# Two score groups set side by side and three transposes moved to the DMA crossbar, in an RWKV-5 and feed-forward kernel on one core

## The chip, the core and the metric

The kernel runs on one core of a Trainium2 chip. A core has five engines with instruction streams of their own: TensorE (PE in the profile; its weight loads are PEld), VectorE (DVE), ScalarE (ACT), GpSimd (POOL) and SyncE (SP), which here only issues DMAs. The metric is the device time of one execution in microseconds (us); lower is better. A change is told by the median of several runs.

## What is computed

Inputs are r, k, v of 4 batches x 8 heads x 768 steps x 48 (float32), w and u (8 x 48), and the two weights of the feed-forward part (384 x 2048 and 2048 x 384).

```python
for t in range(S):                     # per batch and head; state is 48 x 48
    cur = outer(u * k[t], v[t])
    y[t] = r[t] @ (state + cur)
    state = w[:, None] * state + outer(k[t], v[t])
x = y of all heads side by side        # 3072 tokens x 384
h = maximum(x @ w_in, 0)
out = (h * h) @ w_out                  # 3072 x 384, float32
```

## The kernel before

The 4 x 768 tokens are cut into 24 units of 128 tokens of one batch, all 8 heads in each. The list `UNITS` gives unit i's batch and its place in time. Units 0 to 3 are worked in pairs by code of their own (`PAIRED = 4`); the text is about units 4 to 23. The recurrence within a unit is done as matmuls: scores r k^T with the decays multiplied in beforehand, masked, times v, plus r times the state that the batch's earlier unit left.

For a unit i the steps are these (the letter after the colon in `ORDER` names the engine: A ScalarE, D VectorE, G GpSimd, P TensorE, S SyncE):

- `ld.r`, `ld.k`, `ld.v` (L321): loads from HBM, one DMA each.
- `rh`, `kh` (L340, L337): r and k times their decays, into the two halves of tile rk, bf16.
- rk transposed into tile rkT, in one of two ways. Either `T` (L398, eight 128x128 transposes on TensorE into a PSUM bank) and `Tc` (a copy from the bank, L251 on ScalarE, L253 on VectorE); or `XB` (L404), one DMA that turns the tile through the DMA crossbar. Before the change units 4, 5 and 9 go by `T`, the other seventeen by `XB`.
- `A` (L411): eight matmuls with 48 rows each, two rows groups of the array in turn, into two PSUM banks. `Bm` (L419, VectorE, two per unit): the banks times the mask, into Bm.
- `P0`, `P1`, `du`, `dv` (L343, L347, L350, L355): the term with u, kept apart from the matmuls. `vb` (L251 or L253): v in bf16.
- `Y` (L450, L452): state times r and Bm times v, into a bank. `xs` (L475, VectorE): that plus dv, in bf16.
- `U` (L463), `ts`, `S` (L481, L484): the state's step.
- xs transposed into its half of the group's tile xT, again in one of two ways. Either `X` (L489, three transposes on TensorE) and `xTc` (a copy from the bank, L251 or L253); or `xX` (L496), one DMA through the crossbar. Before the change units up to 15 go by `X`, units 16 to 23 by `xX`.

The feed-forward part works on groups of one or two units (`GROUPS`: units 4 and 5 are group 3, 8 and 9 group 5, 12 and 13 group 7, 14 and 15 group 8). `F1.g.s` (L505, six matmuls of 128x256 or twelve of 128x128) makes a bank of x @ w_in, `re` (L515 on ScalarE, L517 on VectorE) takes the maximum with 0, `sq` (L522, L524) squares. `F2.i.q` (L533, four matmuls of 128x384) adds a quarter of the second product into a bank of unit i, `os` copies it out of the bank, and `out.i` (L586; L584 for the paired units) stores it, one DMA. Unit 23 is done in column parts (`Fh`, `oh`, `outh`).

What sets the order of the work is one string, `ORDER`. Its words are emitted one after the other, each on its engine, so that every engine's instruction stream is `ORDER` filtered by its letter; nothing is reordered later. After the engine's letter stand the buffers that the step fills: `A.5:P/6/0` puts unit 5's scores into PSUM banks 6 and 0. Waits between engines follow from the tiles and banks that steps share. DMAs of the letters S, A and G are issued by SyncE, ScalarE and GpSimd. SyncE issues nearly all; a step behind a waiting one on its queue waits too.

Of the kernel before, what the change touches and what calls it, by code (L numbers as in the profile page):

```python
# [51 lines left out]
kh.11:D/3 X.7:P/4 U.7:P/5 kh.10:G/5 F2.4.2:P/0 xTc.7:A/2 ts.7:D/0 XB.11:S/2 vb.8:A/0 F1.4.1:P/4 os.4:A/4 S.7:D
F1.4.7:P/5 re.4.1:A/3 P0.10:D/1 du.9:D/3 XB.8:S/3 U.8:P/0 F2.5.2:P/6 re.4.7:A/4 vb.9:G/1 S.6:D F1.4.3:P/4 os.5:A/5
XB.10:S/4 P1.8:D re.4.3:D/0 F1.4.4:P/5 F1.4.0:P/6 re.4.4:A/2 rh.13:D/4 ld.k.13:S/4 F1.4.2:P/4 ts.8:D/0 ld.v.11:S/2
re.4.0:A/5 sq.4.1:D/24 U.9:P/5 ld.v.10:S/3 F1.4.5:P/0 re.4.2:A/1 ts.9:D/1 sq.4.0:A/25 sq.4.3:D/26 A.11:P/1/2 A.9:P/6/4
P0.11:D/2 P1.11:G sq.4.2:A/27 F2.6.0:P/5 ld.r.12:S/4 Bm.9.1:D/2 re.4.5:A/3 F2.6.1:P/5 sq.4.7:A/5 Bm.9.0:D/3
ld.v.12:S/4 dv.9:G sq.4.5:A/7 Bm.11.1:D/5 F1.4.6:P/4 Bm.11.0:D/7 sq.4.4:A/3 du.8:D/4 kh.13:G/4 A.10:P/3/7 A.8:P/0/6
re.4.6:A/5 F2.7.0:P/2 Bm.8.0:D/0 sq.4.6:A/9 ld.k.12:S/5 ld.r.15:S/7 Y.9:P/1 dv.8:D vb.11:A/2 F2.7.2:P/2 Bm.8.1:D/1
S.9:G vb.10:A/3 ld.k.14:S/7 F2.6.3:P/5 out.4:A P1.10:G Y.8:P/4 xs.9:D/3 F2.7.3:P/2 xs.8:D/4 P0.13:G/0 X.9:P/0
Bm.10.1:D/4 X.8:P/6 F2.6.2:P/5 xTc.8:A/0 du.11:D/0 xTc.9:D/0 rh.12:G/0 Y.11:P/1 U.10:P/4 du.10:D/2 dv.10:G out.0:S  # L60
F1.5.7:P/7 dv.11:G Bm.10.0:D/6 F1.5.6:P/6 ld.v.13:S/5 re.5.7:A/0 P1.13:D ld.r.14:S/6 F1.5.3:P/0 xs.11:D/0 re.5.6:A/1
# [10 lines left out]
rh.17:G/1 F2.10.1:P/6 re.6.4:A/2 xs.12:D/2 F2.11.0:P/2 os.9:D/1 sq.6.4:A/21 P0.16:G/0 XB.17:S/3 ts.13:D/1 Y.13:P/1
kh.16:D/5 F2.10.3:P/6 rh.16:G/5 F2.10.2:P/6 xs.13:D/3 out.5:S du.15:D/4 ld.k.18:S/4 F2.10.0:P/6 P1.16:G ld.r.21:S/3
A.15:P/7/5 A.14:P/0/3 ld.r.19:S/2 Bm.15.0:D/5 dv.15:G X.12:P/1 F2.11.1:P/2 ld.r.18:S/5 Bm.15.1:D/7 S.13:G X.13:P/7
F2.11.3:P/2 xTc.12:D/2 xTc.13:A/2 Bm.14.0:D/4 Y.15:P/5 vb.14:G/7 du.14:D/0 F1.7.3:P/1 ld.v.16:S/1 kh.19:G/0 xs.15:D/4
F1.7.2:P/7 re.7.3:A/0 Bm.14.1:D/6 F1.7.6:P/0 out.9:S out.6:S os.8:D/3 re.7.2:A/1 ld.r.20:S/4 sq.7.3:D/17 Y.14:P/5
re.7.6:A/3 P0.21:G/3 dv.14:D du.17:D/2 F1.7.1:P/1 XB.16:S/2 os.10:A/4 X.15:P/3 F1.7.4:P/4 S.12:G xTc.15:D/0 xs.14:D/0
F1.7.5:P/7 ld.k.20:S/5 rh.19:G/0 U.15:P/0 F1.7.7:P/6 re.7.5:A/4 ld.v.17:S/0 ts.15:D/1 X.14:P/3 S.15:G F1.7.0:P/5
re.7.7:A/5 xTc.14:D/0 P0.19:D/2 sq.7.2:A/20 sq.7.6:A/22 F1.8.7:P/7 XB.19:S/4 F1.8.6:P/0 re.7.4:D/2 sq.7.7:A/23
U.14:P/6 rh.21:G/3 out.8:A F1.8.5:P/3 re.8.6:D/0 kh.18:G/4 ld.r.23:S/6 vb.16:A/1 du.16:D/3 F1.8.0:P/4 sq.7.5:A/24  # L80
rh.20:G/6 re.7.0:D/1 F1.8.2:P/0 re.8.7:A/3 rh.18:D/4 ld.v.19:S/3 sq.7.4:A/25 F1.8.4:P/5 re.8.2:A/5 sq.8.2:A/5
# [555 lines left out]
```

## Time and profile before

| | us |
|---|---|
| median of 3 runs | 170.87 (170.55 to 171.42) |
| the profiled execution | 171.19 |
| its span, first to last instruction | 169.5 |
| TensorE busy | 164.2 |
| VectorE busy | 137.1 |
| ScalarE busy | 101.9 |
| GpSimd busy | 99.9 |

The profile is of one execution. The span is what its views cover; about 1.7 us of the execution's own time lie around it. A row of a timeline has the start (us from the span's start), the duration, engine, line, operation, what it writes and reads, and how many instructions were merged into the row. Where a bracket ends the row, it has the idle time of the engine ahead of it and what ended that. Rows of TensorE carry modelled ends that overlap the next row's start. The busy share of an engine is an average over the whole; the 40 slices show it in time, each digit a tenth.

### The profile page before, as it was taken

The page shows a single profiled execution, that of the slowest core. Times are in us where ns is not written, and L with a number is a line of the kernel's source. Part 1 is how long each engine was busy: PE and PEld are TensorE (multiplying, and loading weights), DVE is VectorE, ACT ScalarE, POOL GpSimd, SP SyncE. Part 2 cuts the span into 40 slices and gives each one's busy share as a digit, 9 for nine tenths or more (in the row PEclk, how much of TensorE's full clock was granted, in tenths as well). Part 3 has the DMA queues.
Part 4 walks back from the last instruction along what each step waited for, and adds up shares of the span by engine and source line. Part 5 has one row for each costly group of instructions (what it writes and reads, how often), then busy time and mean ns, then how long its engine had stood idle before and what let it go on. Part 6 is the DMA issues. An engine that isn't in the chain of part 4 may idle for free.

```text
span 169.5 us, 4602 instructions
## 1 busy us (share of the span) xinstructions
PE 164.2 (97%) x1828; PEld 125.4 (74%) x1828; DVE 137.1 (81%) x255; ACT 101.9 (60%) x190; POOL 99.9 (59%) x122
## 2 busy tenths in 40 slices
PE   4999999999999999999999999999999999999993
...
DMA packets 96137, 27.56 MB, mean 163 GB/s; under 512 B 90642, under 2 KB 96020, under 8 KB 96116
## 3 DMA queue, kind: packets, MB, share of 16 engines
...
q0 software_dynamic: 2816, 3.54, 11.5%
...
q8 instruction: 14, 0.23, 0.6%
q14 instruction: 7, 0.06, 0.1%
...
## 4 chain that ended last, share of the span: by engine, by line
PE 95%; ACT 1%; DVE 1%; issue 1%; ACTq 0%
PE bank L505 37%; PE bank L533 36%; PE bank L411 3%; PE bank L463 2%; PE bank L452 2%; PE bank L364 2%; PE bank L489 2%; PE bank L450 2%; PE bank L547 2%; PE bank L440 1%; PE bank L269 1%; DVE Bm L392 1%; PE bank L303 1%; PE bank L272 1%; PE bank L398 1%; PE bank L428 1%
## 5 line engine op out<-in xcount | busy, mean ns | idle before, releaser
L505 PE MATMUL bank<-xT,W 128*128 128x256 bf16 (+1 forms) x672 | 70.0, 257 | 0.0
L533 PE MATMUL bank<-W,hq 128*128 128x384 bf16 x368 | 68.9, 326 | 0.0
L505 PEld LDWEIGHTS <-W 128*128 128x128 bf16 x672 | 56.9, 98 | 7.7
L515 ACT ACTIVATE hr<-bank 128x512 bf16<-128x512 f32 x67 | 38.7, 594 | 36.4 <-PE bank L505 27.8
L533 PEld LDWEIGHTS <-hq 128*128 128x128 bf16 x368 | 33.8, 98 | 18.2
L522 ACT ACTIVATE hq<-hr 128x512 bf16<-128x512 bf16 x70 | 41.0, 626 | 3.4 <-DVE hr L517 2.8
L419 DVE TENSOR_TENSOR Bm<-bank,maskJT 128x512 bf16<-128x512 f32 x40 | 25.7, 682 | 2.7 <-PE bank L411 2.7
L355 POOL TENSOR_TENSOR dv<-ldv,du 128x384 f32<-128x384 f32 (+1 forms) x18 | 15.9, 891 | 16.2 <-DVE du L350 11.3
L517 DVE TENSOR_SCALAR hr<-bank 128x512 bf16<-128x512 f32 x29 | 19.7, 686 | 6.6 <-PE bank L505 4.5
L347 POOL TENSOR_TENSOR P<-P,ub 128x384 f32<-128x384 f32 x15 | 16.0, 1070 | 13.1 <-DVE P L343 12.7
L340 POOL TENSOR_TENSOR rk<-ldr,Wt 128x384 bf16<-128x384 f32 x15 | 16.4, 1101 | 0.0
L343 POOL TENSOR_TENSOR P<-ldr,ldk 128x384 f32<-128x384 f32 x13 | 13.3, 1023 | 1.5 <-DMA ldk<-in_k_dram 1.2
L524 DVE TENSOR_TENSOR hq<-hr 128x512 bf16<-128x512 bf16 x26 | 12.4, 490 | 2.0 <-ACT hr L515 1.8
L484 POOL TENSOR_TENSOR S0W<-ts,WLm 128x384 bf16<-128x384 f32 x10 | 10.9, 1091 | 4.4 <-DVE ts L481 3.6
L475 DVE TENSOR_TENSOR xs<-bank,dv 128x384 bf16<-128x384 f32 x20 | 11.1, 553 | 3.0 <-PE bank L452 1.1
L337 POOL TENSOR_TENSOR rk<-ldk,Wk 128x384 bf16<-128x384 f32 x12 | 12.3, 1032 | 1.4 <-DMA ldk<-in_k_dram 1.4
L350 DVE TENSOR_REDUCE du<-P 128x8 f32<-128x384 f32 x24 | 12.9, 542 | 0.0
L253 DVE COPY os<-bank 128x384 f32<-128x384 f32 x11 | 6.1, 551 | 6.9 <-PE bank L533 6.9
L481 DVE TENSOR_TENSOR ts<-bank,S0W 128x384 f32<-128x384 f32 x16 | 8.7, 550 | 1.2 <-POOL S0W L484 0.8
L452 PE MATMUL bank<-vb,Bm 128*128 128x48 bf16 x160 | 9.5, 183 | 0.0
L251 ACT COPY os<-bank 128x384 f32<-128x384 f32 (+2 forms) x14 | 6.3, 458 | 4.5 <-PE bank L533 2.5
L452 PEld LDWEIGHTS <-Bm 128*128 128x128 bf16 x160 | 8.2, 96 | 1.0
...
## 6 DMA issues: line engine op xcount, KB each, us to landing
...
```

The source lines that it names most:

```text
L340: e.tensor_mul(rk[slot[f"rk{i}"]][:, 0, :, 0:D], loaded("r", i), Do.factor("t", i % 2 if i < PAIRED else 2))
L343: e.tensor_mul(P0b[slot[f"P{i}"]], loaded("r", i), loaded("k", i))
L347: e.tensor_mul(t, t, bank("bu")[:, 0 : H * D].rearrange("p (h d) -> p h d", h=H) if i in EARLY_U else ub)
L350: e.tensor_reduce(dub[slot[f"dv{i}"]], P0b[slot[f"P{i}"]], axis=mybir.AxisListType.X, op=ALU.add)
L355: e.tensor_mul(dv_of(i) if i < PAIRED else dvb[slot[f"dv{i}"]], loaded("v", i), t)
L419: e.tensor_mul(Bmb[slot[f"Bm{i}{h}"]], heads(bank(f"bA{i}{h}"), 128), mask_b)
L452: e.matmul(y[:, hc, D * h : D * (h + 1)], m[h][:, hc, :], vb[:, 2 * hc + h, :], start=(c == 0), stop=True, skip_group_check=True,)
L505: e.matmul(hp[:, fi, :], W1[f // 4][:, c, 256 * (f // 2 % 2) : 256 * (f // 2 % 2 + 1)].rearrange("p (m j) -> p j m", j=2)[:, f % 2, :], xt ...
L515: e.activation(hr, hp, AF.Relu)
L517: e.tensor_scalar_max(hr, hp, 0.0)
L522: e.activation(hq, hr, AF.Square)
L533: e.matmul(bank(f"bO{i}")[:, 0:d_model], hqb[slot[f"hq{g},{f // m}"]][:, at : at + L], W2[q][:, f % 4, :], start=(seen[i] == 1 and f % 4 = ...
```

## The change

Only words of `ORDER` change; no function does.

- `A.5` stands right behind `A.4`, in banks 1 and 2 instead of 6 and 0. `A.6` stands right behind `A.7`, in banks 1 and 2 instead of 6 and 5, and `Bm.6.0`, `Bm.6.1` stand right behind `Bm.7.0`, ahead of `re.3.5` and `P1.9` on VectorE.
- Unit 9's r and k: `T.9` and `Tc.9` go, `XB.9` comes, on SyncE behind `ld.v.8`, into the same buffer.
- The x of units 12 and 15: `X.12`, `xTc.12`, `X.15`, `xTc.15` go; `xX.12` and `xX.15` come, on SyncE, each behind the unit's `xs` in `ORDER`.
- The stores `out.12`, `out.15` and `out.16` go from SyncE's queue to GpSimd's, at the same places in `ORDER`.

The diff, with the string's line breaks moved so that each part is seen by itself:

```diff
 P1.4:D du.4:D/4 sq.1.1:D/9 A.4:P/5/0
+A.5:P/1/2
 sq.2.6:A/10 re.2.3:A/5 sq.2.3:A/11 F2.0.1:P/4 sq.2.0:A/12 F2.0.3:P/4 vb.4:G/4 Bm.4.1:D/0 Bm.4.0:D/1 sq.2.7:A/13 P0.5:D/1
-A.5:P/6/0
 Bm.5.1:D/2 sq.2.4:A/14 F2.1.1:P/5 Bm.5.0:D/3 F2.1.2:P/5
...
 os.2:D/3 du.6:D/2 A.7:P/5/6
+A.6:P/1/2
 ld.k.11:S/2 re.3.7:A/2 vb.7:G/7 F1.3.5:P/4 Bm.7.1:D/0 sq.3.2:A/20 rh.8:G/2 F2.4.0:P/0 ld.k.10:S/3 Bm.7.0:D/1
+Bm.6.0:D/2 Bm.6.1:D/3
 sq.3.7:A/21 rh.9:G/1 S.3:G F2.4.1:P/0 re.3.5:D/1 ld.v.8:S/0
+XB.9:S/0
 P1.9:D
-A.6:P/6/5 Bm.6.0:D/2
 dv.6:G
-T.9:P/4 Bm.6.1:D/3
 out.2:S F2.4.3:P/0
-Tc.9:A/0
 rh.11:G/3 F2.5.0:P/6 ld.v.9:S/1 P0.8:D/4 sq.3.4:A/22 Y.6:P/5 rh.10:G/5 ld.r.13:S/5 sq.3.5:A/23 F2.5.3:P/6 xs.6:D/1 Y.7:P/4 X.6:P/5
...
 rh.17:G/1 F2.10.1:P/6 re.6.4:A/2 xs.12:D/2
+xX.12:S/2
 F2.11.0:P/2 os.9:D/1 sq.6.4:A/21 P0.16:G/0 XB.17:S/3
...
 Bm.15.0:D/5 dv.15:G
-X.12:P/1
 F2.11.1:P/2 ld.r.18:S/5 Bm.15.1:D/7 S.13:G X.13:P/7 F2.11.3:P/2
-xTc.12:D/2
 xTc.13:A/2 Bm.14.0:D/4 Y.15:P/5 vb.14:G/7 du.14:D/0 F1.7.3:P/1 ld.v.16:S/1 kh.19:G/0 xs.15:D/4
+xX.15:S/0
 F1.7.2:P/7 re.7.3:A/0 Bm.14.1:D/6 F1.7.6:P/0 out.9:S out.6:S
...
 F1.7.1:P/1 XB.16:S/2 os.10:A/4
-X.15:P/3
 F1.7.4:P/4 S.12:G
-xTc.15:D/0
 xs.14:D/0
...
-out.15:S
+out.15:G
 re.10.7:A/1 dv.21:G
...
-out.12:S
+out.12:G
...
 out.17:G F1.12.0:P/6 F1.11.4:P/0
-out.16:S
+out.16:G
```

More of the change, by code (lines that the diff above doesn't have):

```diff
@@ L52 @@
[L52 to L61, printed above, removed]
@@ L72 @@
[L72 to L81, printed above, removed]
@@ new lines @@
+rh.8:G/2 F2.4.0:P/0 ld.k.10:S/3 Bm.7.0:D/1 Bm.6.0:D/2 Bm.6.1:D/3 sq.3.7:A/21 rh.9:G/1 S.3:G F2.4.1:P/0 re.3.5:D/1
+ld.v.8:S/0 XB.9:S/0 P1.9:D dv.6:G out.2:S F2.4.3:P/0 rh.11:G/3 F2.5.0:P/6 ld.v.9:S/1 P0.8:D/4 sq.3.4:A/22 Y.6:P/5
+rh.10:G/5 ld.r.13:S/5 sq.3.5:A/23 F2.5.3:P/6 xs.6:D/1 Y.7:P/4 X.6:P/5 kh.8:G/2 F2.5.1:P/6 xs.7:D/2 xTc.6:A/2 kh.11:D/3
+X.7:P/4 U.7:P/5 kh.10:G/5 F2.4.2:P/0 xTc.7:A/2 ts.7:D/0 XB.11:S/2 vb.8:A/0 F1.4.1:P/4 os.4:A/4 S.7:D F1.4.7:P/5
+re.4.1:A/3 P0.10:D/1 du.9:D/3 XB.8:S/3 U.8:P/0 F2.5.2:P/6 re.4.7:A/4 vb.9:G/1 S.6:D F1.4.3:P/4 os.5:A/5 XB.10:S/4
@@ new lines @@
+ld.k.14:S/7 F2.6.3:P/5 out.4:A P1.10:G Y.8:P/4 xs.9:D/3 F2.7.3:P/2 xs.8:D/4 P0.13:G/0 X.9:P/0 Bm.10.1:D/4 X.8:P/6
+F2.6.2:P/5 xTc.8:A/0 du.11:D/0 xTc.9:D/0 rh.12:G/0 Y.11:P/1 U.10:P/4 du.10:D/2 dv.10:G out.0:S F1.5.7:P/7 dv.11:G
+Bm.10.0:D/6 F1.5.6:P/6 ld.v.13:S/5 re.5.7:A/0 P1.13:D ld.r.14:S/6 F1.5.3:P/0 xs.11:D/0 re.5.6:A/1 ld.v.15:S/6
+du.13:D/1 F2.7.1:P/2 rh.15:G/6 ld.k.15:S/6 ts.10:D/1 F1.5.4:P/3 re.5.4:A/4 XB.13:S/5 kh.12:G/0 X.11:P/7 Y.10:P/1
+F1.5.1:P/6 S.10:G xs.10:D/1 sq.5.4:A/4 F1.5.5:P/4 re.5.3:D/3 ld.k.17:S/0 sq.5.6:D/2 X.10:P/3 F1.5.0:P/1 xTc.10:A/1
@@ new lines @@
+ld.r.17:S/0 os.7:D/6 xTc.11:A/1 F1.5.2:P/0 re.5.1:D/2 P0.12:D/3 re.5.5:A/5 F1.6.1:P/3 P0.14:D/4 XB.12:S/1 re.5.2:A/4
+vb.12:G/4 U.12:P/2 rh.14:D/2 F1.6.7:P/7 sq.5.2:A/1 kh.15:G/6 sq.5.5:A/0 F1.6.0:P/6 S.8:D ld.k.16:S/1 P0.15:G/2
+sq.5.3:A/6 F1.6.2:P/4 P1.12:D re.6.7:A/1 ld.k.19:S/3 F2.9.2:P/0 re.5.0:A/4 P1.15:G sq.5.7:A/14 U.11:P/7 sq.5.1:D/10
+F2.9.1:P/0 re.6.0:A/5 ld.k.21:S/2 F2.9.3:P/0 sq.6.0:A/13 ts.11:D/1 S.11:G F1.6.5:P/1 re.6.2:A/3 P1.14:D F1.6.3:P/6
+out.7:A ld.r.16:S/1 ts.12:D/0 re.6.5:D/0 sq.5.0:A/11 F1.6.6:P/7 kh.14:G/2 os.6:A/7 F2.8.2:P/4 vb.13:A/5 re.6.6:D/2
@@ new lines @@
+A.14:P/0/3 ld.r.19:S/2 Bm.15.0:D/5 dv.15:G F2.11.1:P/2 ld.r.18:S/5 Bm.15.1:D/7 S.13:G X.13:P/7 F2.11.3:P/2 xTc.13:A/2
+Bm.14.0:D/4 Y.15:P/5 vb.14:G/7 du.14:D/0 F1.7.3:P/1 ld.v.16:S/1 kh.19:G/0 xs.15:D/4 xX.15:S/0 F1.7.2:P/7 re.7.3:A/0
+Bm.14.1:D/6 F1.7.6:P/0 out.9:S out.6:S os.8:D/3 re.7.2:A/1 ld.r.20:S/4 sq.7.3:D/17 Y.14:P/5 re.7.6:A/3 P0.21:G/3
+dv.14:D du.17:D/2 F1.7.1:P/1 XB.16:S/2 os.10:A/4 F1.7.4:P/4 S.12:G xs.14:D/0 F1.7.5:P/7 ld.k.20:S/5 rh.19:G/0 U.15:P/0
+F1.7.7:P/6 re.7.5:A/4 ld.v.17:S/0 ts.15:D/1 X.14:P/3 S.15:G F1.7.0:P/5 re.7.7:A/5 xTc.14:D/0 P0.19:D/2 sq.7.2:A/20
@@ new lines @@
+sq.8.0:A/27 sq.8.1:D/0 ld.v.21:S/4 re.8.3:A/1 A.17:P/3/1 dv.16:G A.16:P/5/0 Bm.17.1:D/2 F2.13.1:P/7 sq.8.3:A/4
+Bm.16.0:D/3 sq.8.4:A/1 dv.17:G F2.12.0:P/6 sq.8.5:A/6 Bm.17.0:D/0 F2.15.1:P/4 P0.20:G/1 Bm.16.1:D/1 F2.15.3:P/4
+du.19:D/1 kh.20:G/6 Y.16:P/1 os.11:D/0 F2.15.0:P/4 xs.16:D/1 kh.21:G/3 out.11:A Y.17:P/5 xX.16:S/1 vb.18:A/3
+A.19:P/3/0 xs.17:D/2 dv.19:G A.18:P/2/1 F2.15.2:P/4 Bm.18.0:D/5 vb.19:G/2 xX.17:S/1 F2.12.3:P/6 Bm.19.0:D/7 P1.20:G
+F2.14.0:P/5 os.15:D/6 os.13:A/5 ld.k.23:S/6 out.3:A rh.23:G/2 Bm.19.1:D/4 F2.14.2:P/5 ld.v.23:S/6 Bm.18.1:D/6 U.19:P/2
@@ new lines @@
+S.14:G F2.14.3:P/5 ld.r.22:S/7 ld.k.22:S/7 U.17:P/3 Y.19:P/4 vb.20:G/4 ts.17:D/0 U.18:P/7 Y.18:P/0 S.17:D F1.9.2:P/1
+du.18:D/4 F2.12.2:P/6 dv.18:G ts.19:D/0 F1.9.7:P/3 xs.19:D/3 xX.19:S/2 P0.23:G/0 xs.18:D/4 re.9.7:A/3 F1.9.6:P/2
+F1.9.5:P/4 re.9.2:A/2 xX.18:S/2 F1.9.3:P/0 sq.9.2:A/2 re.9.6:A/0 F1.9.4:P/3 XB.20:S/5 kh.23:D/2 sq.9.6:D/14
+F2.14.1:P/5 re.9.4:A/1 du.20:D/0 F1.9.1:P/1 out.13:S re.9.5:A/4 P0.22:D/2 XB.21:S/6 sq.9.7:A/10 re.9.3:D/5 F1.9.0:P/2
+P1.22:G sq.9.5:A/11 F1.10.5:P/3 sq.9.3:D/13 os.14:A/1 vb.23:G/5 dv.20:D re.9.0:A/2 F2.16.3:P/4 P1.23:G ld.v.22:S/7
@@ new lines @@
+F2.17.2:P/2 xs.20:D/0 sq.10.2:A/21 sq.10.4:D/17 Y.21:P/1 xX.20:S/0 sq.10.0:A/20 F2.17.1:P/2 xs.21:D/1 sq.10.7:A/7
+F2.19.1:P/3 re.10.1:A/0 xX.21:S/0 F2.18.2:P/6 os.17:A/3 out.12:G sq.10.1:A/9 A.23:P/0/7 A.22:P/1/5 os.16:A/0
+Bm.23.0:D/4 F2.18.1:P/6 Bm.22.0:D/7 F2.18.3:P/6 Bm.22.1:D/5 F2.18.0:P/6 F1.11.2:P/2 Y.22:P/4 re.11.2:D/3 F1.11.0:P/0
+xs.22:D/2 F2.19.0:P/3 Bm.23.1:D/6 xX.22:S/0 F1.11.1:P/1 os.18:D/2 F1.11.5:P/5 re.11.0:D/2 out.18:G F1.11.3:P/2
+re.11.5:D/5 Y.23:P/4 sq.11.5:D/22 F2.19.2:P/3 xs.23:D/3 re.11.3:A/4 sq.11.3:A/23 xX.23:S/1 sq.11.2:A/0 F1.12.1:P/7
@@ new lines @@
+out.17:G F1.12.0:P/6 F1.11.4:P/0 out.16:G re.12.1:D/1 F2.21.1:P/5 re.12.0:A/0 F1.11.6:P/4 re.11.1:A/5 sq.12.0:D/27
+re.11.4:D/4 F1.12.3:P/2 sq.11.1:D/1 sq.11.4:A/6 F1.13.1:P/7 re.12.3:D/3 F1.12.2:P/6 sq.12.3:D/3 F2.20.1:P/1
+re.12.2:A/0 F1.13.2:P/0 F1.13.0:P/2 F2.19.3:P/3 sq.11.0:D/26 re.13.2:D/5 sq.13.2:A/24 re.13.1:D/4 F2.21.2:P/5
+sq.12.2:A/25 F1.11.7:P/6 re.11.6:A/3 F2.22.2:P/0 sq.11.6:A/4 re.11.7:D/2 re.13.0:A/5 F2.20.2:P/1 sq.12.1:D/5
+sq.11.7:D/10 sq.13.0:A/14 F1.13.3:P/7 sq.13.1:D/18 F2.20.3:P/1 re.13.3:A/0 F2.20.0:P/1 Fh.23.2.0:P/4 os.20:A/5
```

74 lines of the change are left out of this document (27 added, 47 removed).

## The prediction

> **What bounds the kernel now.** I read the busy shares, the slices and the chain of work that ended last, then TensorE's timeline.
>
> ```profile
> PE 164.2 (97%) x1828; PEld 125.4 (74%) x1828; DVE 137.1 (81%) x255; ACT 101.9 (60%) x190; POOL 99.9 (59%) x122
> ...
> PE   4999999999999999999999999999999999999993
> ...
> PE 95%; ACT 1%; DVE 1%; issue 1%; ACTq 0%
> ```
>
> TensorE is 97% busy, is full in every slice but the first and the last, and carries 95% of the chain. So a microsecond taken off TensorE is a microsecond off the end, as long as nobody else is late in its place. VectorE is the one to fear:
>
> ```profile
> 50.00:100.00 50.00, 50.00 (x563) 38.23 (x561) 46.97 (x82) 31.82 (x60) 40.59 (x42) 1.00 0.97 189
> ```
>
> This row of the table by stage (TensorE, weight loads, VectorE, ScalarE, GpSimd, granted clock, DMA share, GB/s) says that from 50 to 100 us VectorE works 46.97 of 50 us and the DMA engines are 97% full. TensorE's clock is granted whole (1.00), so durations can be compared as they stand.
>
> **The change part by part.** First TensorE's own time, from its timeline. Only starts are used, since the ends are modelled and overlap: from one row's start to the next is what a group costs.
>
> ```profile
> 48.37 0.82 PE L505 MATMUL bank<-xT,W 128*128 128x256 bf16 x6
> 49.12 0.40 PE L411 MATMUL bank<-rkT 48*128 48x128 bf16 x8
> 49.45 0.83 PE L505 MATMUL bank<-xT,W 128*128 128x256 bf16 x6
> 50.11 1.46 PE L533 MATMUL bank<-W,hq 128*128 128x384 bf16 x8
> 51.51 0.40 PE L411 MATMUL bank<-rkT 48*128 48x128 bf16 x8
> 51.84 0.62 PE L398 MATMUL bank<-identity,rk 128*128 128x128 bf16 x8
> 52.30 1.46 PE L533 MATMUL bank<-W,hq 128*128 128x384 bf16 x8
> ```
>
> These are A.7 (49.12) and A.6 (51.51), each alone, and T.9 (51.84). Six F1 matmuls take 0.66 us with another F1 or F2 behind them (49.45 to 50.11) but 0.75 with an A behind them (48.37 to 49.12): entering an A costs 0.09. The A itself costs 0.33 (49.12 to 49.45; 51.51 to 51.84). One alone is 0.42, two are 0.84. A pair that already stands side by side:
>
> ```profile
> 62.54 0.62 PE L411 MATMUL bank<-rkT 48*128 48x128 bf16 x16
> 63.09 1.48 PE L533 MATMUL bank<-W,hq 128*128 128x384 bf16 x8
> ```
>
> Sixteen take 0.55; with 0.09 for entering, 0.64. Each pairing saves 0.84 - 0.64 = 0.20, and there are two (4/5 and 7/6): **0.40 us**. T.9 goes: 51.84 to 52.30, **0.46 us**. The transposes X.12 and X.15:
>
> ```profile
> 98.51 0.33 PE L489 MATMUL bank<-identity,xs 128*128 128x128 bf16 x3
> 98.68 1.47 PE L505 MATMUL bank<-xT,W 128*128 128x256 bf16 x12
> ...
> 100.16 0.82 PE L505 MATMUL bank<-xT,W 128*128 128x256 bf16 x6
> 100.93 0.34 PE L489 MATMUL bank<-identity,xs 128*128 128x128 bf16 x3
> 101.10 2.13 PE L505 MATMUL bank<-xT,W 128*128 128x256 bf16 x18
> ```
>
> X.15 is the row at 98.51 and costs 0.17, X.12 the same: **0.34 us**. The six F1 before X.14 take 0.77 (100.16 to 100.93) instead of 0.66, because xs.14 sits on VectorE behind xTc.15; that copy goes, and I count 0.05 of the 0.11 as won. TensorE is relieved of 0.40 + 0.46 + 0.34 + 0.05 = **1.25 us**. Now what eats it.
>
> *Place one, F2.3.2.* The first pairing wants 0.20 here.
>
> ```profile
> 33.89 2.71 ACT L522 ACTIVATE hq<-hr 128x512 bf16<-128x512 bf16 x5
> ```
> ```profile
> 36.24 1.46 PE L533 MATMUL bank<-W,hq 128*128 128x384 bf16 x8
> ```
>
> ScalarE squares five tiles without a break; the fourth, which F2.3.2 (36.24) reads, ends about 36.1 (four fifths of 2.71 after 33.89), and the change moves nothing ahead of it. TensorE can come at most 0.14 earlier: 0.06 lost. A.5 itself needs Tc.5, which is done before A.4 starts, and banks 1 and 2, long free.
>
> *Place two, X.6.* TensorE now wants to be ahead by 0.14 + 0.20 + 0.46 = 0.80. VectorE:
>
> ```profile
> 49.56 1.29 DVE L419 TENSOR_TENSOR Bm<-bank,maskJT 128x512 bf16<-128x512 f32 x2
> ...
> 51.36 0.68 DVE L347 TENSOR_TENSOR P<-P,ub 128x384 f32<-128x384 f32 x1
> ...
> 53.16 0.94 DVE L343 TENSOR_TENSOR P<-ldr,ldk 128x384 f32<-128x384 f32 x1
> 54.24 0.56 DVE L475 TENSOR_TENSOR xs<-bank,dv 128x384 bf16<-128x384 f32 x1
> ```
> ```profile
> 54.99 0.33 PE L489 MATMUL bank<-identity,xs 128*128 128x128 bf16 x3
> ```
>
> From 49.56 to 54.10 VectorE runs seven instructions end to end (four Bm, re.3.5, P1.9, P0.8), then xs.6, which X.6 (54.99) waits for. The change shuffles the seven (Bm.6 ahead of re.3.5 and P1.9) and removes none; they can start only 0.14 earlier, with A.7. So P0.8 ends at 53.96, xs.6 at 53.96 + 0.56 = 54.52, X.6 starts no earlier than 54.55: ahead by 0.44, not 0.80. **0.36 us lost.** re.3.5 comes a microsecond later than before, but its sq.3.5 finds ScalarE free of Tc.9.
>
> What is uncertain is the seven's length, for P1.9 moves from beside one GpSimd instruction to beside another:
>
> ```profile
> 52.69 2.27 POOL L340 TENSOR_TENSOR rk<-ldr,Wt 128x384 bf16<-128x384 f32 x2
> ```
> ```profile
> L343 DVE TENSOR_TENSOR P<-ldr,ldk x11: 542/552/1252, 6.5 to 125.6; 128x384 f32<-128x384 f32 x11
> ```
>
> Such an instruction takes 0.54 undisturbed (least of eleven); P0.8, beside the GpSimd pair at 52.69, took 0.94, and P1.9 0.68. If both take 0.54 the seven are 0.54 shorter, and the whole 0.80 arrives. If P1.9 too takes 0.94, 0.44 - 0.26 = 0.18 is left. I keep the durations as they are, the middle. The Trainium skill, page "SBUF — State Buffer", section "Who interferes with whom", says that a VectorE instruction with two SBUF inputs contends with a GpSimd instruction that reads SBUF, and that issue order decides who waits; the 0.94 agrees, and by it the 0.18 is as possible as the 0.80.
>
> *After that* TensorE gains 0.17 at X.12, 0.17 at X.15 and the 0.05. Net: 0.44 + 0.34 + 0.05 = 0.83, say **0.85 us**; ends 0.57 and 1.21.
>
> *The three crossbar transfers* hang on SyncE's queue, one DMA each.
>
> ```profile
> L496 SPq DMA_TRANSPOSE xT<-xs x8: 1178/1180/1281, 115.1 to 148.2; - x8
> ...
> DMA to landing us min/median/max: 2.3/2.3/2.9
> ```
> ```profile
> DMA to landing us min/median/max: 3.1/3.6/4.8
> ```
>
> The first answer is of the eight xX, the second of the seventeen XB. XB.9 is issued about 51.3 and lands by 56.1 at worst; A.9 runs after 62.54. Behind it stand out.2, ld.v.9 and ld.r.13, each some 1.3 us later, and then a pause of SyncE:
>
> ```profile
> 53.61 0.70 SPq L321 DMA_DIRECT2D ldr<-in_r_dram  x1
> 56.48 2.64 SPq L404 DMA_TRANSPOSE rkT<-rk  x2
> ```
> ```profile
> 57.29 0.72 POOL L253 CAST vb<-ldv 128x384 bf16<-128x384 f32 x1
> 63.49 1.00 POOL L347 TENSOR_TENSOR P<-P,ub 128x384 f32<-128x384 f32 x1 [5.48 <-DVE P L343]
> ```
>
> The 2.2 us between 54.31 and 56.48 take the 1.3 up; vb.9 (57.29), which needs ld.v.9, has 5.48 us of idle GpSimd behind it. Cost 0. xX.12 fills a like pause of SyncE ahead of 90.63:
>
> ```profile
> 87.82 0.59 SPq L321 DMA_DIRECT2D ldv<-in_v_dram  x1
> 90.63 1.28 SPq L404 DMA_TRANSPOSE rkT<-rk  x1
> ...
> 95.50 1.26 SPq L321 DMA_DIRECT2D ldv<-in_v_dram  x1
> ```
> ```profile
> 95.98 0.55 DVE L475 TENSOR_TENSOR xs<-bank,dv 128x384 bf16<-128x384 f32 x1
> ```
>
> xX.15 needs xs.15 (done 96.53) and SyncE, free after ld.v.16 at 96.76. It lands 2.3 to 2.9 later, 99.1 to 99.7. Group 8 starts at 101.10 + 0.66 = 101.76, in the new run about 100.9: hidden, with 1.2 us to spare. The stores:
>
> ```profile
> 134.93 1.66 POOL L355 TENSOR_TENSOR dv<-ldv,du 128x384 f32<-128x384 f32 x2 [1.24 <-DVE du L350]
> ...
> 146.14 1.19 POOL L586 DMA_DIRECT2D out_dram<-os  x2 [8.26 <-DVE os L253]
> ```
>
> GpSimd spends 0.6 on a store (1.19 for two). out.15 goes into the 1.24 us of idle ahead of dv.21, out.12 into the 8.26, out.16 behind the last. What they free on SyncE nobody waited for. Cost and gain 0; without that cover dv.21 would be 0.6 late.
>
> **The sum.** The profiled execution took 171.19 us: 169.5 of span and 1.7 around it. The median of the runs is 170.87, 0.3 lower; the saving is the same. 170.87 - 0.85 = **170.0 us**. Half a per cent, 0.85 us here, is about what a measurement of this kernel can tell from no change, so the forecast lies on that border.
>
> **The rivals.**
> *Full gain.* VectorE's seven run undisturbed, X.6 waits for nobody: 0.80 + 0.34 + 0.05 = 1.2, **169.7**. For: 0.54 is what such instructions usually take. Against: GpSimd is busy all through.
> *Swallowed.* The edits do what they say on TensorE, but the freed time becomes waits: 0.18 at X.6, and xX.15 at its slowest takes what X.12 and X.15 gave. About 0.2 saved, **170.7**. For: VectorE's 46.97 of 50.
> *Slower: xX.15 late.* If xX.12 does not fit its pause, SyncE, which issues without a break from 90.63 to 96.76, is 1.2 later and starts xX.15 at 98.0; the DMA engines are full, and it may take XB's longest 4.8 us: landing 102.8 against 101.76, 1.1 later than before: **172.0**. It decides from a landing after 101.76 (no gain) and costs over 0.85 from 102.6. Against: all eight xX landed within 2.9. The Trainium skill, page "VectorE: DVE Perf Modes", section "Rules for kernel authors", advises TensorE for a 128x128 transpose where PSUM will do, and the crossbar otherwise; that speaks against this change, and the trace agrees on latency alone (0.17 on TensorE against 2.3 to land).
>
> **How the numbers follow.** Forecast (0.6 to 1.0 saved) 0.52, of which 0.32 falls beyond the border and 0.20 within; full gain 0.25; swallowed 0.10; slower 0.13. So faster 0.57, same 0.30, slower 0.13. Range: from the full gain with the runs' own scatter (170.55 to 171.42, some 0.4 down) 169.3, up to no gain at all, 170.9, which leaves out the slower case.
>
> **What would show it.** In the new trace: two L411 rows of sixteen near 33 and 49 us; no L398 near 52; after 49 us X.6 right behind the end of xs.6, with VectorE full up to it and TensorE waiting about 0.35 (if it does not wait, the full gain); xX.15 landed before group 8's first F1; no new idle ahead of dv.21. Wrong it would be if TensorE idles ahead of group 8, or if loads behind XB.9 hold up GpSimd past 63.5.

## The result and the profile after

The changed kernel took 172.18 us, the median of 15 runs (170.96 to 176.42); the kernel before, run beside it, 171.25 (also 15). The ratio of the two is **1.0043, 95% interval 1.0022 to 1.0064**: about 0.7 us slower, where 0.85 us faster was forecast. In the profiled execution, 176.09 us with a span of 174.4, TensorE's matmuls up to about 24 us ran at half their rate (0.107 us from start to start instead of 0.056), as in some executions of the other versions; the ratios leave such executions out, the medians hold all runs. The traces below are therefore compared from the start of `A.4` on, which lies ahead of all that the change touches (32.66 us before, 36.82 after).

The head of the page, busy times and TensorE's slices:

```profile
PE 167.8 (96%) x1814; PEld 128.0 (73%) x1814; DVE 138.1 (79%) x253; ACT 101.0 (58%) x189; POOL 101.1 (58%) x125
...
PE   4999999999999799999999999999999999999993
```

TensorE has 14 matmuls fewer, and a slice that is no longer full: the fourteenth, from 56.7 to 61.0 us. A hole of this kind was not there before. First the savings, in TensorE's timeline (start, duration, line, tiles, how many):

```profile
36.82 0.62 PE L411 MATMUL bank<-rkT 48*128 48x128 bf16 x16
...
53.18 0.62 PE L411 MATMUL bank<-rkT 48*128 48x128 bf16 x16
53.73 0.83 PE L505 MATMUL bank<-xT,W 128*128 128x256 bf16 x6
54.40 2.76 PE L533 MATMUL bank<-W,hq 128*128 128x384 bf16 x16
```

Both pairs stand as rows of sixteen, the second takes 0.55 (53.18 to 53.73), and no `T.9` breaks the sixteen F2 behind it. Then the hole:

```profile
58.34 0.21 PE L452 MATMUL bank<-vb,Bm 128*128 128x48 bf16 x2
59.71 0.34 PE L489 MATMUL bank<-identity,xs 128*128 128x128 bf16 x3 [1.16 <-DVE xs L475]
```

`X.6` starts 1.37 after the last part of `Y.7`, where one such part takes 0.05: TensorE waits 1.32, for `xs.6`. VectorE's timeline has the reason:

```profile
53.62 2.48 DVE L419 TENSOR_TENSOR Bm<-bank,maskJT 128x512 bf16<-128x512 f32 x4
56.02 0.68 DVE L517 TENSOR_SCALAR hr<-bank 128x512 bf16<-128x512 f32 x1
56.62 1.29 DVE L347 TENSOR_TENSOR P<-P,ub 128x384 f32<-128x384 f32 x1
57.84 1.35 DVE L343 TENSOR_TENSOR P<-ldr,ldk 128x384 f32<-128x384 f32 x1
59.11 1.01 DVE L475 TENSOR_TENSOR xs<-bank,dv 128x384 bf16<-128x384 f32 x2
```

The seven instructions from the first `Bm` to the end of `P0.8` (57.84 + 1.35 = 59.19) took 5.57 us; before, 4.54 (49.56 to 54.10). The four `Bm` and `re.3.5` are what they were. **`P1.9` took 1.29 instead of 0.68, `P0.8` 1.35 instead of 0.94**: 1.02 of the 1.03. GpSimd's rows beside them:

```profile
56.50 0.99 POOL L340 TENSOR_TENSOR rk<-ldr,Wt 128x384 bf16<-128x384 f32 x1
```
```profile
57.46 1.31 POOL L340 TENSOR_TENSOR rk<-ldr,Wt 128x384 bf16<-128x384 f32 x1
```

These are `rh.11` and `rh.10`. `P1.9` began 0.12 after `rh.11` and ended at 57.91, 0.42 after its end (57.49); `P0.8` began 0.38 after `rh.10` and ended 0.42 after its end (58.77). The second place where TensorE waits, ahead of group 8:

```profile
105.33 0.82 PE L505 MATMUL bank<-xT,W 128*128 128x256 bf16 x6
106.52 1.25 PE L505 MATMUL bank<-xT,W 128*128 128x256 bf16 x10 [0.37 <-ACT hq L522]
```
```profile
100.37 0.55 DVE L475 TENSOR_TENSOR xs<-bank,dv 128x384 bf16<-128x384 f32 x1
```
```profile
101.15 1.28 SPq L321 DMA_DIRECT2D ldv<-in_v_dram  x1
102.52 1.41 SPq L496 DMA_TRANSPOSE xT<-xs  x1
```
```profile
DMA to landing us min/median/max: 3.9/3.9/3.9
```

Six F1 take 0.66, so the next could start at 105.99; it starts at 106.52, 0.53 late. The bracket names ScalarE, but group 8 reads what `xX.15` brings. `xs.15` is done at 100.92; SyncE is busy up to `ld.v.16` and takes `xX.15` up at 102.52, 1.60 later; it lands 3.9 after that (the last row is of this transfer alone), at 106.4, and group 8 starts 0.13 behind the landing. What came of the other parts:

```profile
138.56 0.61 POOL L586 DMA_DIRECT2D out_dram<-os  x1
139.86 1.65 POOL L355 TENSOR_TENSOR dv<-ldv,du 128x384 f32<-128x384 f32 x2 [0.69 <-DVE du L350]
...
142.73 0.59 POOL L586 DMA_DIRECT2D out_dram<-os  x1
151.05 1.60 POOL L586 DMA_DIRECT2D out_dram<-os  x3 [7.72 <-DVE os L253]
```

```profile
62.33 0.50 POOL L253 CAST vb<-ldv 128x384 bf16<-128x384 f32 x1 [1.33 <-DMA ldv<-in_v_dram]
68.14 1.00 POOL L347 TENSOR_TENSOR P<-P,ub 128x384 f32<-128x384 f32 x1 [5.31 <-DVE P L343]
```

A store costs GpSimd 0.6, and GpSimd still idles 0.69 ahead of `dv.21` and 7.72 later on. `vb.9` (62.33) waits 1.33 for `ld.v.9`, behind which GpSimd idles 5.31 for VectorE.

TensorE's ledger, by the starts of its rows counted from `A.4`, after against before (minus: earlier):

| stretch | forecast | measured |
|---|---|---|
| first pairing, up to `A.7` | -0.14 | -0.10 |
| second pairing and `T.9`, up to `X.6` | -0.66 | -0.66 |
| wait for VectorE ahead of `X.6` | +0.36 | **+1.32** |
| `X.6` to group 4's first F1 | 0 | -0.06 |
| `X.12`, `X.15` and the wait ahead of `X.14` | -0.39 | -0.42 |
| wait ahead of group 8's first F1 | 0 | **+0.53** |
| wait ahead of group 10's first F1 | 0 | +0.16 |
| sum | -0.83 | +0.77 |

The last eight matmuls (Fh) start at 166.09 before and 171.00 after: +0.75 from `A.4`, which agrees with the ratio.

### The profile page after: what moved, and what is told of

Same layout as the page of the kernel before. It is cut to its first block, busy times and chain, and to the rows that moved or that the text cites. A ratio compares the mean times of both kernels' runs of the same rounds, so it can differ in the third digit from the quotient of the medians.

```text
span 174.4 us, 4577 instructions
## 1 busy us (share of the span) xinstructions
PE 167.8 (96%) x1814; PEld 128.0 (73%) x1814; DVE 138.1 (79%) x253; ACT 101.0 (58%) x189; POOL 101.1 (58%) x125
## 3 DMA queue, kind: packets, MB, share of 16 engines
q10 hardware_dynamic: 884, 1.18, 2.0%
## 4 chain that ended last, share of the span: by engine, by line
PE 92%; DVE 4%; ACT 2%; issue 1%; ACTq 0%
PE bank L505 36%; PE bank L533 33%; PE bank L463 3%; PE bank L411 3%; PE bank L364 2%; PE bank L452 2%; PE bank L489 2%; PE bank L450 2%; PE bank L547 2%; PE bank L440 1%; PE bank L384 1%; DVE Bm L419 1%; PE bank L269 1%; PE bank L303 1%; PE bank L272 1%; PE bank L428 1%
## 5 line engine op out<-in xcount | busy, mean ns | idle before, releaser
L505 PE MATMUL bank<-xT,W 128*128 128x256 bf16 (+1 forms) x672 | 71.5, 261 | 0.4 <-ACT hq L522 0.4
L505 PEld LDWEIGHTS <-W 128*128 128x128 bf16 x672 | 58.1, 100 | 8.6 <-DVE xT L253 0.6
L251 ACT COPY xT<-bank 128x384 bf16<-128x384 bf16 x8 | 3.7, 479 | 10.8 <-PE bank L489 10.8
```

Source lines behind the costliest of these rows:

```text
L505: e.matmul(hp[:, fi, :], W1[f // 4][:, c, 256 * (f // 2 % 2) : 256 * (f // 2 % 2 + 1)].rearrange("p (m j) -> p j m", j=2)[:, f % 2, :], xt ...
```

## The experiments

**Theory.** A VectorE instruction with two inputs in SBUF (the core's memory for tiles, beside the PSUM banks) that starts while GpSimd works on SBUF stands still until that GpSimd instruction ends, and then needs 0.4 more. The change let `P1.9` and `P0.8` each begin just behind the start of a GpSimd instruction. Separately, `xX.15` lands late because the DMA engines are full there. **Rivals:** `XB.9`, which now runs through the crossbar in the same stretch, slows VectorE or GpSimd; the pairing itself makes VectorE late, whatever the order; the seven are long for reasons that any order has. Edits are shown against the changed kernel. The results of all runs, with the waits of TensorE at the three places that matter and its lead (start counted from `A.4`, against before; minus is earlier):

| run | at `X.6` | group 8 | group 10 | lead at group 4 | lead at the end | us, median of all runs | ratio to before, 95% |
|---|---|---|---|---|---|---|---|
| changed kernel | 1.32 | 0.53 | 0.16 | +0.50 | +0.75 | 172.18 | 1.0043 (1.0022 to 1.0064) |
| e1 | 0.37 in `Y.6` | 0.99 | 0 | -0.46 | +0.10 | 171.46 | 1.0029 (1.0008 to 1.0050) |
| e2 | 0 | 0.69 | 0 | -0.83 | +0.25 | 171.39 | 1.0033 (1.0003 to 1.0063) |
| e3 | 1.31 | 0 | 0 | +0.49 | +0.56 | 173.45 | 1.0015 (0.9996 to 1.0034) |
| e4 | 0 | 0 | 0.20 | -0.83 | +0.23 | 171.03 | 1.0010 (0.9994 to 1.0027) |
| e5 | 0 | 1.05 | 0.18 | -0.82 | -0.03 | 170.93, one run | |
| e6 | 0.36 in `Y.6` | 0 | 0.17 | -0.47 | -0.74 | 170.77 | 0.9981 (0.9960 to 1.0003) |
| e7 | 0.37 in `Y.6` | 0 | 0 | -0.45 | -0.72 | 170.37 | 0.9974 (0.9958 to 0.9991) |
| e8 | 1.06 at `T.9` | 0 | 0 | +0.84 | +0.71 | 175.83, one run | |
| e9 | 0.37 in `Y.6` | 0 | 0.26 | -0.46 | -0.48 | 171.06 | 1.0004 (0.9986 to 1.0023) |
| e10 | 0.96 in `Y.6`, 0.35 | 0 | 0 | +0.48 | +0.21 | 175.44, one run | |
| e11 | 0 | 0 | 0.30 | -0.78 | -0.44 | 174.59, six runs | |
| e12 (e7 again) | 0.36 in `Y.6` | 0 | 0.20 | -0.46 | -0.53 | 170.54 | 0.9976 (0.9960 to 0.9992) |
| e13 (e9 again) | 0.36 in `Y.6` | 0 | 0.23 | -0.47 | -0.51 | 170.76 | 0.9997 (0.9984 to 1.0011) |

Each lead is of one execution and can differ from what the ratio says by half a microsecond (e9: -0.48 against about +0.07). Many of the ratios' intervals overlap. So the causes below are told apart by waits and durations in the traces, and a ratio decides only where its interval is clear of the other.

**e1: VectorE's order as before, all else changed.**

```diff
-Bm.6.0:D/2 Bm.6.1:D/3
 ... re.3.5:D/1 ... P1.9:D
+Bm.6.0:D/2 Bm.6.1:D/3
```

> The changed kernel with VectorE's order as before in one place: Bm.6.0 and Bm.6.1 behind P1.9 again. Theory (shared port): P1.9 and P0.8 read two SBUF tiles; begun while a GpSimd instruction runs, each ends about 0.42 us after that one ends; behind the two Bm.6 both fall early into a GpSimd instruction (1.29 and 1.35 us instead of 0.68 and 0.94). In the old order they take about 0.7 and 0.9 again, X.6 waits 0.3 instead of 1.2, about 0.9 us faster than the changed kernel, some 170.9. Rival (crossbar): XB.9's traffic in the full DMA stretch slows what is there; then nothing changes, 171.9.

VectorE's timeline, and where TensorE stands:

```profile
50.80 0.75 DVE L347 TENSOR_TENSOR P<-P,ub 128x384 f32<-128x384 f32 x1
...
52.67 0.93 DVE L343 TENSOR_TENSOR P<-ldr,ldk 128x384 f32<-128x384 f32 x1
```
```profile
52.80 0.20 PE L452 MATMUL bank<-vb,Bm 128*128 128x48 bf16 x1 [0.20 <-DVE Bm L419]
...
101.40 1.36 PE L505 MATMUL bank<-xT,W 128*128 128x256 bf16 x11 [0.82 <-DMA xT<-xs]
```

The products are back at 0.75 and 0.93 and TensorE is 0.46 early at group 4: the 0.44 of the forecast, with its 0.36 of waiting as 0.37, spent inside `Y.6` on the second `Bm.6` rather than at `X.6`. `XB.9` is still there, so it is not what slowed the products, and neither is the pairing. The lead at group 4 is 0.96 better than the changed kernel's, the 0.9 expected; by the whole time the two can't be told apart (1.0029 and 1.0043, overlapping), because the gain ends ahead of group 8, where TensorE now waits 0.99 for the DMA by name. The earlier TensorE is, the longer it waits: the landing sets the time. `xs.15` is done at 95.35 here, SyncE takes `xX.15` up at 96.49, and its landing takes (that transfer alone):

```profile
DMA to landing us min/median/max: 4.8/4.8/4.8
```

Busy times by stretch of the kernel before (TensorE, weight loads, VectorE, ScalarE, GpSimd, clock, **DMA share**, GB/s), where `xX.15` now runs and where the eight `xX` of the forecast's row ran:

```profile
95.00:105.00 10.00, 10.00 (x117) 8.82 (x116) 10.00 (x18) 6.92 (x14) 8.94 (x10) 1.00 1.08 220
115.00:150.00 35.00, 35.00 (x389) 27.08 (x387) 27.63 (x49) 18.25 (x36) 16.87 (x20) 1.00 0.62 133
```

The eight of before land 2.3 to 2.9 after their issue, `xX.15` 3.9 or 4.8 after it. That the load is the reason is borne out by `xX.12`, which thirteen of the profiles have: it lands after 2.3 to 2.9 where the DMA share between its issue and its landing is 0.24 to 0.59, and after 3.3 to 4.1 where it is 0.89 to 1.08. But load is not all: in the changed kernel `xX.19` (127.11) lands only after 3.8, at a share of 0.41. What holds that one up no run here shows. What sets group 8's start is clear: it lies 0.13 to 0.14 behind the landing of `xX.15` in the changed kernel, e1, e2 and e5.

**e2: the two products moved to where GpSimd is idle.**

```diff
-P1.9:D  -P0.8:D/4
+P1.9:D  (ahead of du.9)   +P0.8:D/4  (ahead of P1.8)
```

> The changed kernel with P1.9 and P0.8 moved on VectorE to where GpSimd is idle (right ahead of du.9 and of P1.8). Theory (shared port): each takes 0.54 there, X.6 waits for nobody, 1.2 to 1.3 us are won over the changed kernel up to that point; xX.15 depends on SyncE's queue and not on TensorE, so the wait ahead of group 8 grows from 0.5 to about 1: 170.6 to 171.0. Rival (crossbar): X.6 or its surroundings still wait, 171.5 or more.

```profile
57.14 0.54 DVE L347 TENSOR_TENSOR P<-P,ub 128x384 f32<-128x384 f32 x1
...
58.65 0.55 DVE L343 TENSOR_TENSOR P<-ldr,ldk 128x384 f32<-128x384 f32 x1
```

Both take 0.54 to 0.55 there, `X.6` waits for nobody, and the whole 0.80 arrives (-0.83 at group 4). But the time, 171.39, misses the 170.6 to 171.0 expected, for the work is not gone: VectorE is late a little further on, and TensorE waits 0.69 ahead of `F1.4.2`, then 0.69 ahead of group 8.

**e3: X.15 back on TensorE, VectorE's new order kept.**

```diff
-xX.15:S/0
+X.15:P/3  (behind os.10)   +xTc.15:D/0  (behind S.12)
```

> The changed kernel with unit 15's x turned by TensorE and copied by VectorE again. Theory: the wait of 0.5 us ahead of group 8 goes and 0.17 of transposes come back: 0.3 to 0.4 faster than the changed kernel, 171.5; X.6 still waits 1.2. Rival (the wait is VectorE's, not the transfer's): xs.14 is late again behind xTc.15, no gain, 171.9.

```profile
100.04 0.82 PE L505 MATMUL bank<-xT,W 128*128 128x256 bf16 x6
101.03 0.34 PE L489 MATMUL bank<-identity,xs 128*128 128x128 bf16 x3 [0.17 <-DVE xs L475]
```

The wait ahead of group 8 is gone, so it was `xX.15` and not the ScalarE instruction of the bracket. In its place `X.14` (101.03) comes 0.99 after six F1 that need 0.66: it waits 0.33 for `xs.14`, which stands behind `xTc.15` on VectorE. The gain in the trace is 0.19 (+0.75 to +0.56), less than the 0.3 to 0.4 expected.

**e4: e2 and e3 together.**

> Both mends at once (P1.9 and P0.8 where GpSimd is idle, unit 15's x on TensorE). Theory: the two waits are all that the changed kernel lost, so 0.40 + 0.46 + 0.17 us come through: 1.0 to 1.1 faster than before, about 170.1. Rival: a third loss remains, 170.8 or more.

It does not add up to a faster kernel: a third loss remains, as the rival had it. From TensorE's timeline:

```profile
60.99 0.82 PE L505 MATMUL bank<-xT,W 128*128 128x256 bf16 x6 [0.65 <-DVE hr L517]
```

`F1.4.2` starts 0.81 late, for `re.4.3` behind the moved products. I read this as VectorE being the bound of this stretch wherever the two products stand, so that only the time they lose to GpSimd is to be had; e5, where they take 0.55 in their place and `F1.4.2` waits for nobody, agrees.

**e5: the same place and order, but one SBUF input.** The second factor of `P0.8` and `P1.9` is read from a PSUM bank, which leaves the u-term of units 8 and 9 out.

```diff
-P1.9: P * ub          P0.8: ldr * ldk
+P1.9: P * bank 1      P0.8: ldr * bank 2
```

> The changed kernel, but P1.9 and P0.8 take their second factor from the PSUM banks 1 and 2 instead of SBUF, in the same places; the u-term of units 8 and 9 is thereby left out. Theory (shared port): with one SBUF input each they do not wait for GpSimd, take 0.55 us instead of 1.29 and 1.35, and X.6 waits for nobody: from A.4 to F1.4.1 0.8 us shorter than before, where the changed kernel was 0.5 longer. Rival (the order alone: more VectorE work ahead of xs.6): the two still take over 0.9 and X.6 waits about a microsecond.

VectorE's rows (the kernel has six more lines, so its lines are shifted), and GpSimd's:

```profile
52.27 0.55 DVE L351 TENSOR_TENSOR P<-P,bank 128x384 f32<-128x384 f32 x1
52.73 0.55 DVE L344 TENSOR_TENSOR P<-ldr,bank 128x384 f32<-128x384 f32 x1
```
```profile
52.16 1.96 POOL L340 TENSOR_TENSOR rk<-ldr,Wt 128x384 bf16<-128x384 f32 x2
```

Under the same `rh.11` (52.16 to 53.16), `P1.9` begins 0.11 after its start, as in the changed kernel (0.12), and both take 0.55, and GpSimd's pair takes 1.96 instead of 2.27. This is what tells the theory from its rivals: place, order, pairing and crossbar are as in the changed kernel, and the stall is gone. The Trainium skill, page "SBUF — State Buffer", section "Who interferes with whom", says that a VectorE instruction with two SBUF inputs contends with a GpSimd instruction that reads SBUF, that one with at most one does not (outside the 2-port modes), and that issue order decides which of the two is blocked. The runs agree on each: 1.29 and 1.35 against 0.55; `P1.9` waits behind `rh.11`, and `rh.10`, begun behind `P1.9`, takes 1.31 instead of 0.99.

**e6: e1, with xX.15 ahead of ld.v.16 on SyncE.**

```diff
-ld.v.16:S/1 kh.19:G/0 xs.15:D/4 xX.15:S/0
+kh.19:G/0 xs.15:D/4 xX.15:S/0 ld.v.16:S/1
```

> The changed kernel with VectorE's old order (Bm.6 behind P1.9) and with xX.15 ahead of ld.v.16 on SyncE's queue. Theory: xX.15 lands late (4.8 us from issue) because it stands behind loads in the full DMA stretch; one load fewer ahead of it lands it 1.0 to 1.2 us earlier, and the wait of 1.0 ahead of group 8 goes. From A.4 on 0.7 to 0.8 shorter than before: 170.2 to 170.4. Rival (the transfer itself takes that long in that stretch): the wait stays near 1.0, 171.1.

```profile
95.83 1.64 SPq L496 DMA_TRANSPOSE xT<-xs  x1
```

Here it is issued 0.1 after `xs.15` (done 95.72) and, counted from `A.4`, 1.0 sooner than in e1; group 8 waits for nobody, and TensorE is 0.90 early there, more than the forecast's 0.83. Its landing is not in the trace; group 8's start at 100.78 only says that it took less than 5.0. So the earlier issue is enough, and whether the transfer itself became faster stays open. Group 10 takes 0.17 back, and the time, 170.77, is above the 170.2 to 170.4 expected.

**e7: e1, with X.15 on TensorE.**

```diff
(e1's edit and e3's)
```

> The changed kernel with VectorE's old order and unit 15's x on TensorE again: only the two pairings, XB.9 and xX.12 are left. Theory: ahead by 0.45 at F1.4.1 and 0.17 more with X.12, less a wait of 0.2 to 0.3 for xs.14 ahead of X.14: 0.3 to 0.4 shorter than before, about 170.7. Rival: another wait takes it, 171.0 or more.

The fastest: 170.37 us, ratio 0.9974 (0.9958 to 0.9991); 170.7 was expected. TensorE's timeline ahead of group 8:

```profile
99.10 0.82 PE L505 MATMUL bank<-xT,W 128*128 128x256 bf16 x6
99.76 0.33 PE L489 MATMUL bank<-identity,xs 128*128 128x128 bf16 x3
99.92 1.25 PE L505 MATMUL bank<-xT,W 128*128 128x256 bf16 x10
```

`X.14` follows six F1 after 0.66, without the 0.11 of before and the 0.33 of e3, and group 8's first F1 runs straight on in the row of ten.

**e8: before, with the second pairing alone.** Unit 6's scores beside unit 7's and its masked products ahead of `re.3.5` and `P1.9`; `T.9` stays, nothing goes to the crossbar.

```diff
+A.6:P/1/2  (behind A.7)   +Bm.6.0:D/2 Bm.6.1:D/3  (behind Bm.7.0)
-A.6:P/6/5 Bm.6.0:D/2 ... Bm.6.1:D/3
```

> The kernel before, with only A.6 moved beside A.7 (banks 1 and 2) and both Bm.6 ahead of re.3.5 and P1.9; T.9 stays on TensorE, no crossbar transfer is added. Theory (shared port): P1.9 and P0.8 take some 1.3 us each all the same, and from A.4 to F1.4.1 it is 0.4 to 0.6 us longer than before. Rival (crossbar): without XB.9 the loss is gone, and that stretch is 0.1 to 0.2 shorter.

```profile
56.65 0.61 PE L398 MATMUL bank<-identity,rk 128*128 128x128 bf16 x8 [0.90 <-DVE hr L517]
```
```profile
56.51 1.21 DVE L347 TENSOR_TENSOR P<-P,ub 128x384 f32<-128x384 f32 x1
57.65 1.35 DVE L343 TENSOR_TENSOR P<-ldr,ldk 128x384 f32<-128x384 f32 x1
```

Without `XB.9` the products are as slow as with it, so the crossbar is out as a cause. The loss of TensorE (+0.84) is of another kind here and says nothing on `X.6`: `T.9` needs bank 4, which `re.3.5`, now behind two more `Bm`, has not read yet. The pairing needs `T.9` gone.

**e9: e7, with the three stores back on SyncE.**

```diff
-out.15:G  -out.12:G  -out.16:G
+out.15:S  +out.12:S  +out.16:S
```

> The kernel e7 with the three stores back on SyncE's queue. All theories: nobody waits for these stores, so nothing changes: 170.4, and no stretch of TensorE differs by more than 0.1 us. If GpSimd's stores had a price or a gain of their own, it shows here.

I expected no difference, and got 171.06 against 170.37, on another chip; hence e12 and e13 below.

**e10: e7, with re.3.5 and P1.9 changed round on VectorE.**

```diff
-re.3.5:D/1 ... P1.9:D
+P1.9:D re.3.5:D/1
```

> The kernel e7 with re.3.5 and P1.9 changing places on VectorE: the same seven instructions, P1.9 0.6 us earlier. Theory (shared port): P1.9 now begins just after GpSimd's S.3 and ends 0.42 after it, 1.35 us instead of 0.75; P0.8, pushed 0.6 later, begins just after rh.10 and takes about 1.3 instead of 0.94; X.6 comes some 0.95 later and the stretch from A.4 to F1.4.1 is about 0.5 longer than before instead of 0.45 shorter. Rival (only the amount of VectorE work counts): nothing changes.

VectorE and GpSimd:

```profile
54.67 1.34 DVE L347 TENSOR_TENSOR P<-P,ub 128x384 f32<-128x384 f32 x1
...
57.73 1.29 DVE L343 TENSOR_TENSOR P<-ldr,ldk 128x384 f32<-128x384 f32 x1
```
```profile
54.60 1.00 POOL L484 TENSOR_TENSOR S0W<-ts,WLm 128x384 bf16<-128x384 f32 x1
```

A swap of two neighbours, with the same work, turns a lead of 0.45 into a loss of 0.48. `P1.9` now begins 0.07 after `S.3` instead of 0.67, and takes 1.34 instead of 0.75, ending 0.41 after `S.3` (55.60); that makes `P0.8` later against `rh.10`, and it takes 1.29. The theory forecast this from the phase alone, with about the right size.

**e11: e3, with P1.9 alone moved ahead of du.9.**

```diff
-xX.15:S/0  -P1.9:D
+X.15:P/3  +xTc.15:D/0  +P1.9:D  (ahead of du.9)
```

> The changed kernel with its own order of the Bm, unit 15's x on TensorE, and P1.9 alone moved to where GpSimd is idle (ahead of du.9). Theory: six instructions instead of seven ahead of xs.6; P0.8 begins just after rh.11 and takes 1.3, X.6 is still 0.3 earlier than in e7; later P1.9 costs VectorE 0.55, of which 0 to 0.3 reaches TensorE: from A.4 on 0.7 to 0.9 shorter than before, 170.2 to 170.4. Rival (VectorE's total bounds this stretch, not the place): no better than e7, or worse.

It has no ratio. In the trace it is between e4 and e7: -0.78 at group 4, 0.21 of waiting ahead of `F1.4.2`, then 0.30 ahead of group 10; -0.44 at the end, no better than e7 and less than the 0.7 to 0.9 expected.

**e12 and e13: e7 and e9 again, side by side on one chip.**

> The same kernel as the one with unit 6's masked products behind P1.9 and X.15 on TensorE, now side by side on one chip with its twin that has the three stores on SyncE. If what separated the two (170.37 and 171.06, on different chips) is the chip and scatter, both come within 0.15% of each other here, each about 0.25% under the kernel before. If the stores count, this one is 0.3 to 0.6 us below its twin, and group 10's first F1 waits for nobody.

> The twin, with out.12, out.15 and out.16 back on SyncE. If the stores count, TensorE waits about 0.26 ahead of group 10's first F1 again (which no store stands behind in time, so that this wait should not come from them), and the last stores land some 2.4 us after their issue again, not 2.1. If it was scatter, the wait and the late landing are gone or turn up in both.

e7's gain holds (0.9976). The twin is at 0.9997; the two intervals overlap a little, as those of e7 and e9 do, so the moved stores are worth some 0.2% here if anything. The wait ahead of group 10 is 0.20 and 0.23, so it does not come from the stores. It comes from `xX.18`: in e12, e13 and the other runs with a wait of 0.16 or more there, group 10 starts 0.13 to 0.14 behind its landing. SyncE takes `xX.18` up right behind `xX.19`, which holds the queue 2.00 us in e7 and 2.23 in e12; why it does is open. What does go with the stores is the tail. SyncE's last two rows in e12, then in e13:

```profile
core 0 of [0], span 168.9 us
...
165.92 0.81 SPq L561 DMA_DIRECT2D out_dram<-os  x2
```
```profile
core 0 of [0], span 173.5 us
...
170.24 0.81 SPq L561 DMA_DIRECT2D out_dram<-os  x2
```

From the issue of the last stores to the end are 3.0 with the stores on GpSimd and 3.3 with them on SyncE, and the same 0.3 lies between e7 and e9. But the kernel before had its stores on SyncE and 2.9 (166.54 to 169.45). What makes the 0.3 **stays open**.

## Why the prediction was wrong

What held, step by step:

- **TensorE's own time.** Forecast 1.25, less 0.06 at F2.3.2, is 1.19; measured 0.10 + 0.66 + 0.42 = 1.18. Reading it off by starts of rows was right.
- **VectorE as the bound of `X.6`.** Right in the changed kernel, where `X.6` waits for `xs.6`. The 0.36 it was to take is measured as 0.36 to 0.37 in e1, e6, e7, e9, e12 and e13, where VectorE's order is that of before; that it is the same number is partly luck, because there TensorE waits for the second `Bm.6` inside `Y.6`, which the changed order has out of the way. `X.6` then starts 0.07 behind the end of `xs.6` (54.07 and 54.14 in e1).
- **The stores, `XB.9`, `vb.9`.** In the changed kernel none of them held TensorE up: `dv.21` kept 0.69 of idle time ahead of it, and `vb.9` waited 1.33 with 5.31 of idle time behind it. But "cost and gain 0" for the stores is in doubt: the mended kernel is at 0.9974 and 0.9976 with them on GpSimd (e7, e12), and at 1.0004 and 0.9997, no gain, with them on SyncE (e9, e13).

What failed are two steps:

- **"I keep the durations as they are, the middle"**, of the seven. The term was +0.36 and came out as +1.32. It was not the middle of anything: how long these two products take follows from where they start against GpSimd, and the change moved both. The bound, too, was wrong: I let `P1.9` rise to 0.94 at most and left `P0.8` alone, though the row of eleven such instructions beside it showed 1252 ns as its longest. With the rule that e5, e8 and e10 bear out (end of the GpSimd instruction plus 0.42), the traces of before already held the answer: `P0.8` under `rh.11` (52.69 to 53.68) ended at 54.10, 0.42 after it. An instruction that starts right behind the start of a 0.99 us one takes up to 1.4, so the two products had up to 1.4 + 1.4 - 0.68 - 0.94 = 1.2 to lose, over four times the 0.26 that the bound allowed, and that alone would have carried the range past no gain.
- **"It lands 2.3 to 2.9 later"**, of `xX.15`, and SyncE free 0.23 after `xs.15`. It landed 3.9 after its issue, 4.8 in e1, and was issued 1.60 after `xs.15`, 1.14 in e1. I took the landing from eight transfers at 115 to 148 us, where the DMA share is 0.62, for one at 102, where the engines are full; and I took SyncE from the trace of before, where `xX.12` is not in its queue. Nor did `xX.12` fill its pause ahead of 90.63. In the trace of before, `xs.12` ends at 89.95, which leaves 0.68 of the pause for a step of 1.3:

```profile
89.39 0.56 DVE L475 TENSOR_TENSOR xs<-bank,dv 128x384 bf16<-128x384 f32 x1
```

In the changed kernel `XB.17`, the step behind it, starts at 96.08, which is 1.28 later than before, counted from `A.4`:

```profile
94.67 1.30 SPq L496 DMA_TRANSPOSE xT<-xs  x1
96.08 1.24 SPq L404 DMA_TRANSPOSE rkT<-rk  x1
```

The rival that had `xX.15` late named both terms, SyncE 1.2 late and XB's longest 4.8, and put the landing at 102.8 against 101.76; by the clock of the trace of before it came at 102.2 (106.38 - 36.82 + 32.66). I set it aside for the eight short landings, which were of another load, and of which two have no landing in the trace. That its 172.0 stands so near 172.18 is partly luck: it put the whole loss on group 8, where 0.53 came, and nothing on the products.

The two compound badly: because the first loss makes TensorE late, the second shows as only 0.53. Mend the first alone (e1) and the second grows to 0.99. Mend both (e6, e7) and the kernel is 0.7 us ahead in the trace, near the forecast; by e7's ratio of 0.9974 (0.9958 to 0.9991) it is some 0.45 us, half of it. The group 10 wait of 0.16 was in no step; it is again a landing, of `xX.18`, 3.3 after its issue instead of 2.4. Two sums of the prediction are slightly off, without weight for the outcome: 0.80 + 0.34 + 0.05 is 1.19, not 1.21, and 102.8 less 101.76 is 1.0, not 1.1.
